# A planner that schedules forward and backward in turn, and a second layer that trails by six steps in place of five

## The chip, the cores and the metric

The kernel runs on one core of one Trainium2 chip. The metric is device time in microseconds (us) of one execution; lower is better. Medians of several executions are given; all timed runs below were in the fast state, except two single looks whose state is unknown. PE is TensorE's matrix array, PEld its weight loads, DVE is VectorE, ACT ScalarE, POOL GpSimd, SP SyncE (here it only issues DMAs).

## The reference

Two identical layers over a sequence of 2048 rows of width 512. Each layer is attention with a recurrent memory, then a dense block:

```python
x = x + A(layernorm(x)); x = x + B(layernorm(x))      # layer 0
x = x + A(layernorm(x)); x = x + B(layernorm(x))      # layer 1, same weights

def A(x, mem, Wq, Wk, Wv, Wo):                          # 64 segments of 32 rows, 32 heads of 128
    for s in range(64):
        h = concat([mem, x[32*s : 32*s+32]])            # 8 memory rows + 32
        q, k, v = h @ Wq, h @ Wk, h @ Wv
        o = softmax(mask(q @ k.T * scale)) @ v          # per head
        o = o @ Wo
        mem = o[:8]                                     # goes into the next segment
        out[32*s : 32*s+32] = o[8:]

def B(x, w1, w2): return relu(x @ w1) @ w2              # 512 -> 1376 -> 512
```

The memory makes the segments of one layer a chain: segment s+1 cannot compute its queries before segment s has been through Wo. Layer 1 needs finished rows of layer 0, but it has a chain of its own, so the two chains can run side by side.

## The kernel before

In step k the kernel works on segment k of layer 0 and segment k - DELTA of layer 1 together ("double" steps). At either end only one layer is active ("single" steps). Rows are handled in groups of 128, four segments: after the fourth segment of a group its late projection (layer 0 only), its dense block and its layer norm are due. There are 64 + DELTA steps, so DELTA single steps at each end and 64 - DELTA double ones.

No instruction order is written by hand. The kernel records all operations of all steps with engine, cost, what they read and write, and which buffers they take. A list scheduler orders them in Python while the kernel is built, and they are emitted in that order; semaphores keep the result right whatever the order, so the order is a static choice of what each engine does next.

```python
DELTA = 5
LAT = (0.26, 0.16, 0.16, 0.20, 1.70)     # PE ACT DVE POOL SP: us until others see a result
LOOK, TURN, STAY = 0.05, 0.11, 0.5       # TURN: cost of changing PE's tile form

def order(self):
    for o in reversed(self.ops):          # rank: longest path to the end, resources ignored
        o.rank = o.cost + LAT[o.eng] + max((s.rank for s in o.succs), default=0.0)
    ...
    while len(done) < len(self.ops):      # greedy: the engine that can start first, and on it,
        ...                               # of those that can start within LOOK, the highest rank
        o = max((c for c in cand[e] if c.start <= lo + LOOK),
                key=lambda c: (c.rank + (STAY if e == PE and c.tile == tile else 0.0), -c.seq))
        ...
```

The end of a step is the narrow place, where one step's memory becomes the next one's input:

```python
def project(k, act, seg):                 # OT: attention's output, transposed
    for p in range(4): ...                # Wo blocks: 8 matmuls OT x Wo into wo (tile st), per p
    ... ACT copies half of wo to wm, DVE the other half
    ... PE turns wm into columns (selm)   # "memory transposition"
    ... DVE copies the columns into HT of the next step   # "HT copy"; next K/Q matmuls wait for it
    ... DVE adds wo to the residual rows x                # two additions per active layer; not urgent
```

Attention of layer 0 needs V0, rows of values that two DMAs per step bring from vw (`V0[...] <- vw[...]`, issued by SP after all four blocks of values are evacuated, that is, copied out of PSUM). Two more DMAs fill other rows of V0 from vg, values that are computed once per group of rows. The kernel uses eight PSUM banks: five "work", one "st", two "fill"; values, dense and late projection share the two fill banks.

## Time and profile before

1972.38 us (3 runs, 1972.25 to 1975.89). I cut the trace at each HT copy. Steps 8 to 61 are double steps whose order repeats every four, because a group of rows has four segments. I call four such steps a "group", and a group is "clean" if no stretch of it ran at half PE clock.

| | before |
|---|---|
| span of the profiled run | 1973.9 us |
| PE busy / idle in the span | 1730.8 / 243.1 us |
| clean group, mean of six | 110.1 us, PE busy 101.9 |
| steps 8 to 61 | 1506.0 us |
| everything else (start, end, other steps) | 467.9 us |

The stretches view of one clean group, one line per step (32 to 35): length, then busy time of each engine, and the clock that PE was granted (1.00 is full speed).

```profile
core 0: us, PE busy (x) PEld busy (x) DVE busy (x) ACT busy (x) POOL busy (x), PEclk, DMA share, GB/s
958.20:986.50 28.30, 26.69 (x531) 19.30 (x531) 20.13 (x48) 12.84 (x30) 6.89 (x18) 1.00 0.07 14
986.50:1013.70 27.20, 25.86 (x526) 19.13 (x528) 19.64 (x45) 11.62 (x28) 6.03 (x16) 1.00 0.08 15
1013.70:1039.50 25.80, 22.63 (x480) 16.58 (x480) 19.53 (x47) 10.61 (x25) 5.99 (x16) 1.00 0.11 25
1039.50:1068.10 28.60, 26.72 (x524) 18.41 (x524) 19.32 (x44) 10.97 (x26) 6.07 (x18) 1.00 0.08 15
sum 109.90, PE 101.91 PEld 73.43 DVE 78.61 ACT 46.04 POOL 24.98; mean PE 25.48 PEld 18.36 DVE 19.65 ACT 11.51 POOL 6.25
```

PE is busy for 101.9 of 109.9 us and no other engine is close, so PE is the limit, but 8.0 us per group are idle. The third step (34) has the least work and no dense matmuls, and is idle longest. Its end, from the timeline (start, length, engine, line, operation; in brackets the idle time before it and who ended it):

```profile
1033.70 0.32 PE L660 MATMUL work_220<-ident,P_178 128*128 128x80 bf16 x4 [0.59 <-POOL P_178 L650]
...
1035.84 1.15 PE L706 MATMUL st_221<-Wo_sb,OT 128*64 128x512 bf16 x8 [0.53 <-ACT OT L469]
...
1037.03 0.37 ACT L469 CAST wm<-st_221 128x256 bf16<-128x256 f32 x1 [1.24 <-PE st_221 L706]
1037.43 0.42 DVE L471 CAST wm<-st_221 128x256 bf16<-128x256 f32 x1 [1.55 <-ACT wm L469]
...
1037.45 0.21 PE L721 MATMUL work_219<-selm,wm 128*128 128x16 bf16 x2 [0.47 <-ACT wm L469]
1037.88 0.68 DVE L746 TENSOR_TENSOR xg_72<-xg_72,st_221 16x512 f32<-16x512 f32 x1
...
1038.60 0.68 DVE L746 TENSOR_TENSOR xg_75<-xg_75,st_221 32x512 f32<-32x512 f32 x1
1039.31 0.23 DVE L730 CAST HT_172<-work_219 128x64 bf16<-128x64 f32 x1
...
1039.59 0.59 PE L567 MATMUL work_218<-HT_172,Wk_sb 128*128 128x80 bf16 x12 [0.48 <-DVE HT_172 L730]
```

PE waits for the softmax's P, then for the copies of OT, then for wm, and at last for HT. The HT copy stands behind two residual additions of 0.68 us that nobody waits for. In the fourth step PE waits for V0 (called V_181 here):

```profile
1052.51 1.03 PE L517 MATMUL fill_223<-Wv_sb,HT_172 128*64 128x512 bf16 x8
...
1054.19 1.58 SPq L540 DMA_DIRECT2D V_181<-vw  x2
...
1056.70 0.19 PE L679 MATMUL work_217<-PT,V_181 40*128 40x40 bf16 x1 [0.70 <-DMA V_181<-vw]
...
1057.67 0.19 PE L679 MATMUL work_216<-PT,V_181 40*128 40x40 bf16 x1 [0.78 <-DMA V_181<-vw]
```

From the end of the last values block to the attention that waits last it takes about 4.1 us here, and the old order had too little other work to put there.

### The profile page before, as it was taken

What the parts mean: (1) busy time and instruction counts of PE and PEld (TensorE: products, weight loads), DVE (VectorE), ACT (ScalarE), POOL (GpSimd) and SP (SyncE); (2) the same over time, 40 slices, a digit from 0 to 9 for tenths busy, and PEclk for the clock granted to TensorE, in tenths of its full rate; (3) what the DMA queues carried; (4) which work ended last, traced back from release to release, by engine and by line L of the source; (5) the groups of instructions that cost most, each with busy time, mean ns of one, the idle gap of its engine ahead of it and who ended that gap; (6) DMA issues with size and microseconds to landing.
All of it is one profiled execution on the core that took longest, in us unless ns stands there. A gap on an engine that the chain in (4) does not pass through costs nothing.

```text
span 1973.9 us, 78339 instructions
## 1 busy us (share of the span) xinstructions
PE 1730.8 (88%) x34592; PEld 1240.2 (63%) x34624; DVE 1291.7 (65%) x3103; ACT 762.6 (39%) x1843; POOL 419.4 (21%) x1171
## 2 busy tenths in 40 slices
PE   0489889999899989899999989898999999998997
PEld 0356666676566666666666666666666667666665
DVE  0245667776676767766776767776776777676654
ACT  0133334443344434444444434443443434343342
POOL 1211222221221222212221222211222222122111
PEclk9889999999999999999999999999999999999998
DMA  9210000000000000001000000000000000000000
GB/s 335 74 22 16 12 16 16 21 14 17 16 20 15 17 16 15 20 12 22 16 19 16 17 15 17 18 14 19 13 21 12 16 21 14 15 15 19 7 5 5
DMA packets 27429, 49.80 MB, mean 25 GB/s; under 512 B 8560, under 2 KB 15728, under 8 KB 27088
## 3 DMA queue, kind: packets, MB, share of 16 engines
q1 hardware_dynamic: 21520, 31.35, 7.4%
q10 hardware_dynamic: 3824, 6.78, 1.0%
q8 instruction: 271, 4.44, 0.9%
q0 software_dynamic: 1744, 6.65, 0.9%
q14 instruction: 70, 0.57, 0.1%
HBM read 21.70 MB, written 2.10 MB: 12 GB/s over the span
## 4 chain that ended last, share of the span: by engine, by line
PE 70%; DVE 10%; DMA 7%; issue 6%; ACT 4%; SPq 2%; POOL 2%; DVEq 0%; POOLq 0%; ACTq 0%
PE st_221 L706 13%; DMA V_181<-vw 7%; PE fill_222 L517 7%; PE fill_223 L517 7%; PE work_219 L567 6%; PE work_217 L567 6%; PE work_218 L567 5%; PE work_216 L567 5%; PE work_220 L567 5%; PE fill_222 L378 2%; PE fill_223 L378 2%; PE fill_223 L404 2%; SPq L540 2%; DVE wm L471 1%; ACT wm L469 1%
## 5 line engine op out<-in xcount | busy, mean ns | idle before, releaser
L567 PEld LDWEIGHTS <-Wk_sb 128*128 128x128 bf16 x8832 | 344.4, 100 | 94.1 <-issue 78.8
L567 PEld LDWEIGHTS <-Wq_sb 128*128 128x128 bf16 x8832 | 342.9, 100 | 2.4 <-issue 2.1
L706 PE MATMUL st_221<-Wo_sb,OT 128*64 128x512 bf16 x2208 | 310.9, 396 | 25.8 <-ACT OT L469 24.6
L706 PEld LDWEIGHTS <-OT 128*64 128x64 bf16 x2208 | 122.5, 111 | 121.5 <-ACT OT L469 43.0
L650 POOL TENSOR_TENSOR P_175<-es_201,sm_205 128x160 bf16<-128x160 f32 (+1 forms) x138 | 57.2, 435 | 650.1 <-DVE sm_205 L634 372.6
L753 POOL COPY OXb<-OT 128x128 bf16<-128x128 bf16 x256 | 85.9, 336 | 220.0 <-DVE OT L471 182.5
L679 PEld LDWEIGHTS <-V_181 40*128 40x128 bf16 x2048 | 49.6, 94 | 121.1 <-issue 101.9
L628 ACT ACTIVATE es_201<-es_201 128x320 f32<-128x320 f32 (+1 forms) x138 | 62.4, 452 | 99.2 <-DVE es_201 L622 99.1
L378 PEld LDWEIGHTS <-w_sb 128*128 128x128 bf16 (+1 forms) x1408 | 84.1, 102 | 8.0 <-issue 7.4
L650 POOL TENSOR_TENSOR P_176<-es_202,sm_206 128x160 bf16<-128x160 f32 (+1 forms) x138 | 61.0, 463 | 123.9 <-ACT es_201 L628 79.0
L628 ACT ACTIVATE es_202<-es_202 128x320 f32<-128x320 f32 (+1 forms) x138 | 62.2, 451 | 52.1 <-DVE es_202 L622 28.5
L517 PEld LDWEIGHTS <-HT_171 128*64 128x64 bf16 x1120 | 56.7, 110 | 38.6 <-issue 2.0
L471 DVE CAST wm<-st_221 128x256 bf16<-128x256 f32 x68 | 28.9, 424 | 79.5 <-ACT wm L469 78.7
L650 POOL TENSOR_TENSOR P_177<-es_201,sm_207 128x160 bf16<-128x160 f32 (+1 forms) x138 | 57.2, 435 | 103.4 <-DVE sm_207 L634 79.0
L517 PE MATMUL fill_223<-Wv_sb,HT_171 128*64 128x512 bf16 x592 | 77.8, 384 | 0.1
L517 PEld LDWEIGHTS <-HT_172 128*64 128x64 bf16 x1088 | 54.4, 110 | 35.8 <-issue 0.5
L352 PE MATMUL fill_222<-ident,bf_76 128*128 128x128 bf16 x136 | 13.8, 226 | 70.5 <-DVE bf_76 L347 70.5
L517 PE MATMUL fill_222<-Wv_sb,HT_172 128*64 128x512 bf16 x544 | 71.2, 383 | 0.1
L517 PE MATMUL fill_223<-Wv_sb,HT_172 128*64 128x512 bf16 x544 | 70.6, 381 | 0.1
L352 PEld LDWEIGHTS <-bf_76 128*128 128x128 bf16 x256 | 15.4, 100 | 86.7 <-DVE bf_76 L347 75.0
L469 ACT CAST wm<-st_221 128x256 bf16<-128x256 f32 x68 | 25.3, 372 | 114.8 <-PE st_221 L706 114.7
L517 PE MATMUL fill_222<-Wv_sb,HT_171 128*64 128x512 bf16 x528 | 69.1, 383 | 0.1
(299 smaller groups left out, 4230.2 us busy)
## 6 DMA issues: line engine op xcount, KB each, us to landing
V_181<-vw SPq DMA_DIRECT2D x128, 96.0 KB
V_181<-vg SPq DMA_DIRECT2D x128, 64.0 KB
Wk_sb<-in_A_Wk_dram ACTq DMA_DIRECT2D x2, 1024.0 KB
Wv_sb<-in_A_Wv_dram POOLq DMA_DIRECT2D x2, 1024.0 KB, 18.8
Wq_sb<-in_A_Wq_dram SPq DMA_DIRECT2D x2, 1024.0 KB
Wo_sb<-in_A_Wo_dram SPq DMA_DIRECT2D x2, 1024.0 KB
out_dram<-bf_76 SPq DMA_DIRECT2D x16, 128.0 KB
bf_76<-in_A_x_dram SPq DMA_DIRECT2D x15, 128.0 KB
```

The lines of the kernel that those rows point to most:

```text
L378: nc.tensor.matmul(hp[0:fs, fi * 128:(fi + 1) * 128], lhsT=w1_sb[:, c4, fc * 128:fc * 128 + fs], rhs=xnT[:, c4, :], start=(c4 == 0), stop= ...
L404: nc.tensor.matmul(yp[:, :], lhsT=hT[0:fs, fc, :], rhs=w2_sb[0:fs, fc, :], start=(fc == 0), stop=(fc == NFC - 1))
L469: nc.scalar.copy(out=out_, in_=in_)
L471: nc.vector.tensor_copy(out=out_, in_=in_)
L517: nc.tensor.matmul(vp[64 * b:64 * b + 64, :], lhsT=cols[:, c4, :], rhs=Wv_sb[:, c4, n * 512:(n + 1) * 512], start=(c4 == 0), stop=(c4 == N ...
L540: nc.sync.dma_start(out=V0[64 * b + HS:64 * b + L, :, :], in_=vw[64 * b:64 * b + L - HS, :, :])
L567: nc.tensor.matmul(qp[:, hi * 2 * L:hi * 2 * L + n], lhsT=W_sb[:, c4, h * Dh:(h + 1) * Dh], rhs=HT[:, c4, c0:c1], start=(c4 == 0), stop=(c ...
L628: nc.scalar.activation(out=e, in_=e, func=ACTF.Exp, scale=SCALE)
L650: nc.gpsimd.tensor_tensor(out=o, in0=e, in1=s.unsqueeze(3).to_broadcast([128, na, 2, L]), op=ALU.mult)
L679: nc.tensor.matmul(pv[b][:, (2 * hh + a) * L:(2 * hh + a + 1) * L], lhsT=V[R:R + KK[a], p, hh * Dh:(hh + 1) * Dh], rhs=PT[R:R + KK[a], p, ...
L706: nc.tensor.matmul(wo[64 * u:64 * u + 64, :], lhsT=OT[:, h, HS:2 * L], rhs=Wo_sb[:, h, :], start=(p == 0 and hh == 0), stop=(p == 3 and hh ...
L753: nc.gpsimd.tensor_copy(out=OXb[:, 8 * p:8 * p + 8, HS * c:HS * (c + 1)], in_=OT[:, 8 * p:8 * p + 8, 0:HS])
```

## The change

The intent: a priority that knows the resources. The new planner schedules forward with the old longest-path priorities. It then schedules that result backward from its end, honouring engines and buffer reuse, which gives each operation a latest start. Those become the priorities of the next forward pass. Six passes are made and the forward order with the smallest planned end is kept. DELTA becomes 6, so that layer 1 starts a group two steps after layer 0 has finished it. No operation, shape or buffer changes. The diff, cut to its core:

```diff
-DELTA = 5
+DELTA = 6
+PASSES = 6
...
-            o = max((c for c in cand[e] if c.start <= lo + LOOK),
-                    key=lambda c: (c.rank + (STAY if e == PE and c.tile == tile else 0.0), -c.seq))
+            o = min((c for c in cand[e] if c.start <= lo + LOOK),
+                    key=lambda c: (prio[c.seq] - (STAY if e == PE and c.tile == tile else 0.0), c.seq))
...
+                    last = pool.take(b)              # the buffer's former owner:
+                    if last is not None:
+                        o.after += last.users        # o must come after all its users
...
+    def backward(self, total):
+        ...                                          # engines filled from the end; late[] = latest start
+    def order(self):
+        ...
+        for _ in range(PASSES):
+            total = self.forward(prio)
+            if best is None or total < best[0]:
+                best = (total, [(o.start, o.seq) for o in self.ops], [(b, b.i) for b in self.bufs])
+            prio = self.backward(total)
```

## The prediction

> **What bounds the kernel now.** PE is busy 88% of 1973.9 us, VectorE 65%, ScalarE 39%, GpSimd 21% (the page). Cut at each copy of new memory columns into HT, the trace has 69 steps; steps 8 to 61 repeat in fours. A clean group (958.2 to 1068.1, by stretches) takes 109.9 us, PE busy 101.9. PE and its 8.0 us of idle are the limit. That idle, from PE's timeline:
> - V0: attention waits for the DMA from vw: 2.4 us (1.48 in the step with the late values).
> - Step ends: last Wo matmul, wm by ScalarE then VectorE, transposition, HT copy, next K matmul. 1.64 us in one step, 2.6 where two 0.68 us additions stand before the HT copy, 3.3 where a third stands before wm. Fill matmuls leave 3.3 idle.
> - The last Wo block waits for OT copies: 1.36. Transposition of P_178: 0.59..
>
> **What the change does.** No operation, shape or buffer changes; order and step number do.
> (a) DELTA 6: two more single-layer steps, one fewer double step. Single ones took 20.5 us (65, 67), a double one without dense work 25.8 (62): 2 x 20.5 - 25.8 = +15 us.
> (b) A new order, again periodic (read from the built program). Dense work reaches the step that had none; the late projection moves into the following step.
>  - V0: after the last values block PE has about 4.4, 3.0, 3.9 and 4.4 us of work before attention, where the DMA needs 4.2: idle 1.4, was 2.4.
>  - Step ends: one addition before HT in two steps, two in the others, none before wm; more fill: 2.4, was 3.3.
>  - OT: something stands between last attention and last Wo block in every step: 0.3, was 1.36. P_178: 0.3, was 0.59.
>  - Against it: 76 changes of tile form per group, were 72, at 0.11 us (K follows scores by 0.30 us, values by 0.21): +0.4. The Trainium skill, "TensorEngine Tiling (Array Packing)", Key Properties, says that changing the tiling mode drains the engine; the trace agrees (0.1 us). One step runs three attention blocks in a row (six banks wanted of five): +0.45. A transposition of normalised x stands between Wo blocks: +0.3.
>  Net -2 us per group, times 14.5: -29.
> (c) Start (75 us, mostly loading) and tail (about 15 us after the last step): -2.
>
> 1972 + 15 - 29 - 2 = about 1956 us, nearly all of it on the critical path.
>
> **Predicted: 1956 us, 1937 to 1972 eight times in ten. Faster by over 2%: 0.1; within 2%: 0.88; slower: 0.02.**
>
> **What would show it.** PE busy up by 15 to 25 us, to about 1750; its idle down from 243 to about 205. Clean group about 108 us. In the waits: Wo blocks hardly wait for OT, waits for HT shorter, V0's waits near 1.4 per group, most of it in the step after the late values. Dense matmuls in the third and fourth step of a group. Other engines' busy times up by 1 to 2%.
>
> **What would make it wrong.** If the tighter order puts the softmax chain (VectorE, ScalarE, GpSimd) on PE's path, the 2 us go and the extra step alone makes it 1975. If balancing dense work takes more of the 8 us than I count (half, say), it nears 1930. The normalisation inside a step could stall VectorE on GpSimd's power and hold up OT. Clock dips of about 1.5 us (nine steps) differ by run.

## More of the kernel before

From the page: PE's busy time, and the line of the Wo matmuls (after the bars: busy us, mean ns of one, then idle time just before them and who ended it).

```profile
PE 1730.8 (88%) x34592; PEld 1240.2 (63%) x34624; DVE 1291.7 (65%) x3103; ACT 762.6 (39%) x1843; POOL 419.4 (21%) x1171
...
L706 PE MATMUL st_221<-Wo_sb,OT 128*64 128x512 bf16 x2208 | 310.9, 396 | 25.8 <-ACT OT L469 24.6
```

## The result

1901.5 us (median of 6 runs, 1898.01 to 1906.84) against 1971.99 (6 runs): ratio 0.9644, 95% interval 0.9625 to 0.9664. Ratios here are the mean time of one kernel's fast runs over that of the other's in the same rounds, so they are not quite the ratio of the quoted medians. The change saves 70 us, 3.6%; 16 us had been predicted, and the range ended at 1937.

The page after, the same two lines:

```profile
PE 1716.8 (91%) x34902; PEld 1241.2 (65%) x34948; DVE 1292.8 (68%) x3139; ACT 777.2 (41%) x1866; POOL 419.0 (22%) x1179
...
L785 PE MATMUL st_221<-Wo_sb,OT 128*64 128x512 bf16 x2240 | 305.4, 395 | 6.5 <-ACT OT L548 5.9
```

PE makes 0.9% more matmuls and yet is busy 14 us less; the Wo blocks wait 5.9 us for OT in the whole run, where they waited 24.6. Busy time of PE is thus no measure of its work. The Trainium skill ("Perfetto Trace Analysis", Identifying the Most-Contended Engine) warns of the same figure for a related use: matmul busy share is not a good measure of how close a kernel is to the roofline, and the busy share of the weight loads is one of two measures that it puts in its place. Here the weight loads are steady, 1240.2 and 1241.2 us.

A clean group after (steps 28 to 31), by stretches:

```profile
806.30:833.30 27.00, 25.57 (x527) 18.28 (x522) 19.95 (x47) 11.88 (x28) 6.45 (x19) 1.00 0.08 15
833.30:858.90 25.60, 23.98 (x494) 17.59 (x494) 18.61 (x46) 11.10 (x27) 6.15 (x17) 1.00 0.08 15
858.90:884.50 25.60, 24.95 (x527) 19.01 (x529) 19.46 (x46) 12.04 (x28) 6.19 (x17) 1.00 0.08 17
884.50:911.00 26.50, 26.34 (x516) 18.76 (x518) 20.44 (x47) 11.89 (x27) 6.08 (x16) 1.00 0.11 25
sum 104.70, PE 100.83 PEld 73.64 DVE 78.45 ACT 46.90 POOL 24.87; mean PE 25.21 PEld 18.41 DVE 19.61 ACT 11.73 POOL 6.22
```

The group takes 104.7 us, and PE's idle time in it is 3.9 us, half of what it was. The third step, with 2.3 us more PE work than its counterpart before, is 0.2 us shorter. Its end:

```profile
878.54 0.32 PE L739 MATMUL work_220<-ident,P_178 128*128 128x80 bf16 x4
...
880.08 0.84 PE L457 MATMUL fill_223<-xnM_214,w_sb 128*128 128x128 bf16 x12
880.85 1.05 PE L785 MATMUL st_221<-Wo_sb,OT 128*64 128x512 bf16 x8
...
882.06 0.81 PE L483 MATMUL fill_222<-w_sb,hT_215 128*128 128x512 bf16 x3 [0.16 <-issue]
882.35 0.42 DVE L550 CAST wm<-st_221 128x256 bf16<-128x256 f32 x1 [1.56 <-ACT wm L548]
882.71 0.33 PE L800 MATMUL work_217<-selm,wm 128*128 128x16 bf16 x4
...
884.23 0.23 DVE L809 CAST HT_172<-work_217 128x64 bf16<-128x64 f32 x1
...
884.51 0.73 PE L646 MATMUL work_219<-HT_172,Wk_sb 128*128 128x80 bf16 x16 [0.48 <-DVE HT_172 L809]
```

The waits for P, OT and wm are gone: dense work stands in the place of the last two (fill_223 with 12 matmuls, then fill_222), and a Wo block in front of the transposition of P. The wait for HT is as it was. The "issue" of 0.16 us is no wait either: the block on fill_222 has four matmuls and the trace shows three, so one record is missing, and the gap is its time. The group shown has three such gaps, the one before two.

V0's wait in the first step of a group, which now has the late projection:

```profile
819.82 1.05 PE L596 MATMUL fill_223<-Wv_sb,HT_171 128*64 128x512 bf16 x8
...
821.53 1.59 SPq L619 DMA_DIRECT2D V_181<-vw  x2
...
824.00 0.38 PE L853 MATMUL fill_223<-wxs,selx 128*128 128x512 bf16 x1 [0.43 <-ACT wxs L850]
...
824.85 0.19 PE L758 MATMUL work_219<-PT,V_181 40*128 40x40 bf16 x1 [0.35 <-DMA V_181<-vw]
```

Where the 77.6 us between the two profiled spans (1973.9, 1896.3) come from:

| part | before | after | difference |
|---|---|---|---|
| steps 8 to 61 at the pace of their clean groups (13.5 groups of 110.07 and 105.28) | 1485.9 | 1421.3 | -64.7 |
| steps 8 to 61 above that pace | 20.1 | 6.6 | -13.5 |
| all other steps, one more of them after | 467.9 | 468.4 | +0.5 |

The second row is what the groups with a stretch of 3.4 us at half PE clock take more than clean ones: between steps 8 and 61 there are eight such stretches before and four after. Not all of it is lost at half clock. The seven groups of the kernel before that hold the eight stretches have 7.6 us more PE idle time in sum than clean ones, the four after only 0.5, and much of that idle time lies ahead of the stretches. One of them before, from the stretches view (PEclk is the third column from the right):

```profile
496.40:499.80 3.40, 1.85 (x46) 1.12 (x44) 2.84 (x9) 1.70 (x4) 2.03 (x5) 1.00 0.26 53
499.80:503.20 3.40, 3.40 (x38) 1.23 (x34) 1.27 (x3) 1.01 (x2) 1.35 (x6) 0.50 0.00 0
```

In the first 3.4 us PE was idle 1.55 us, in the next it ran at half clock.

### The profile page after: what moved, and what is told of

Same layout as the page of the kernel before. It is cut to its first block, busy times and chain, and to the rows that moved or that the text cites. A ratio compares the mean times of both kernels' runs of the same rounds, so it can differ in the third digit from the quotient of the medians.

```text
span 1896.3 us, 79089 instructions
## 1 busy us (share of the span) xinstructions
PE 1716.8 (91%) x34902; PEld 1241.2 (65%) x34948; DVE 1292.8 (68%) x3139; ACT 777.2 (41%) x1866; POOL 419.0 (22%) x1179
## 4 chain that ended last, share of the span: by engine, by line
PE 77%; DVE 7%; issue 5%; DMA 5%; ACT 3%; POOL 1%; SPq 1%; DVEq 0%; POOLq 0%; ACTq 0%
PE st_221 L785 14%; PE fill_223 L596 11%; PE work_216 L646 7%; PE work_220 L646 6%; PE work_217 L646 6%; PE work_219 L646 6%; PE work_218 L646 6%; PE fill_222 L596 5%; DMA V_181<-vw 5%; PE fill_222 L483 3%; PE fill_223 L457 2%; PE fill_222 L844 1%; SPq L619 1%; DVE wm L550 1%; PE fill_222 L457 1%
## 5 line engine op out<-in xcount | busy, mean ns | idle before, releaser
L646 PEld LDWEIGHTS <-Wk_sb 128*128 128x128 bf16 x8960 | 340.6, 99 | 75.0 <-issue 56.9
L785 PE MATMUL st_221<-Wo_sb,OT 128*64 128x512 bf16 x2240 | 305.4, 395 | 6.5 <-ACT OT L548 5.9
L729 POOL TENSOR_TENSOR P_175<-es_201,sm_205 128x160 bf16<-128x160 f32 (+1 forms) x140 | 60.0, 448 | 726.6 <-DVE sm_205 L713 579.3
L785 PEld LDWEIGHTS <-OT 128*64 128x64 bf16 x2240 | 117.4, 111 | 92.5 <-ACT OT L548 9.7
L832 POOL COPY OXb<-OT 128x128 bf16<-128x128 bf16 x256 | 79.1, 309 | 245.3 <-DVE OT L550 174.8
L596 PE MATMUL fill_223<-Wv_sb,HT_171 128*64 128x512 bf16 x776 | 101.8, 384 | 0.1
L596 PE MATMUL fill_223<-Wv_sb,HT_172 128*64 128x512 bf16 x760 | 99.3, 382 | 0.1
L729 POOL TENSOR_TENSOR P_176<-es_202,sm_206 128x160 bf16<-128x160 f32 (+1 forms) x140 | 64.0, 477 | 83.6 <-DVE sm_206 L713 79.6
L729 POOL TENSOR_TENSOR P_178<-es_202,sm_208 128x160 bf16<-128x160 f32 (+1 forms) x140 | 57.5, 432 | 107.9 <-DVE sm_208 L713 103.3
L483 PE MATMUL fill_222<-w_sb,hT_215 128*128 128x512 bf16 (+1 forms) x277 | 74.4, 381 | 6.5 <-issue 6.5
L729 POOL TENSOR_TENSOR P_177<-es_201,sm_207 128x160 bf16<-128x160 f32 (+1 forms) x140 | 57.5, 432 | 78.0 <-DVE sm_207 L713 64.9
L550 DVE CAST vw<-fill_223 128x512 bf16<-128x512 f32 x97 | 66.5, 686 | 10.0 <-PE fill_223 L596 9.8
```

The costliest lines, as they stand in the source:

```text
L483: nc.tensor.matmul(yp[:, :], lhsT=hT[0:fs, fc, :], rhs=w2_sb[0:fs, fc, :], start=(fc == 0), stop=(fc == NFC - 1))
L550: nc.vector.tensor_copy(out=out_, in_=in_)
L596: nc.tensor.matmul(vp[64 * b:64 * b + 64, :], lhsT=cols[:, c4, :], rhs=Wv_sb[:, c4, n * 512:(n + 1) * 512], start=(c4 == 0), stop=(c4 == N ...
L646: nc.tensor.matmul(qp[:, hi * 2 * L:hi * 2 * L + n], lhsT=W_sb[:, c4, h * Dh:(h + 1) * Dh], rhs=HT[:, c4, c0:c1], start=(c4 == 0), stop=(c ...
L729: nc.gpsimd.tensor_tensor(out=o, in0=e, in1=s.unsqueeze(3).to_broadcast([128, na, 2, L]), op=ALU.mult)
L785: nc.tensor.matmul(wo[64 * u:64 * u + 64, :], lhsT=OT[:, h, HS:2 * L], rhs=Wo_sb[:, h, :], start=(p == 0 and hh == 0), stop=(p == 3 and hh ...
```

## The experiments

Theories at the start. "Order": the new planner makes the gain, DELTA 6 is only a cost. "Room": DELTA 6 makes it, any planner would fill the room. "Both": each alone gains little. About the size: "restart": a wait of PE costs more than the idle time that the profile shows.

All results in one table; "clean" is the mean clean group with PE's idle time in it, "half" the half-clock stretches between steps 8 and 61, "plan" the planner's own end of schedule.

| kernel | median us | ratio to before | clean (idle) | half | plan |
|---|---|---|---|---|---|
| before (three profiles) | 1972 | 1 | 110.1, 109.9, 109.9 (8.2, 7.6, 8.0) | 8, 8, 8 | 1958.5 |
| the change (two profiles) | 1901.5, 1902.2 | 0.9644, 0.9643 | 105.3, 105.5 (4.4, 4.6) | 4, 3 | 1913.0 |
| d6_old | 1941.4 | 0.9838 | 107.9 (5.9) | 4 | 1948.5 |
| d5_new | 1949.7 | 0.9883 | 109.3 (7.5) | 0 | 1938.9 |
| p2 | 1936.0 | 0.9820 | 107.4 (5.6) | 8 | 1927.7 |
| d8_new | 2008.6 | 1.0188 | 109.4 (8.1), one group only | 20 | 1953 |
| before_htfirst | 1937.9 | 0.9828 | 109.1 (7.0) | 3 | |
| before_v0gone | 1938.0 | 0.9818 | 108.9 (7.1) | 3 | |
| before_filled | 1969.4 | 0.9987 | 110.3 (6.9) | 4 | |
| after_htfirst, again as after_htfirst2 | 1890.2, 1879.6 | 0.9584, 0.9543 | 104.3, 104.0 (3.2, 3.3) | 6, 4 | |

### DELTA alone (d6_old) and planner alone (d5_new)

```diff
 # d6_old, on the kernel before        # d5_new, on the changed kernel
-DELTA = 5                             -DELTA = 6
+DELTA = 6                             +DELTA = 5
```

> The old planner with DELTA 6 alone. Theory 'order' (the gain of 70 us is the iterated planning; the sixth step of distance is only a cost): two more single steps against one fewer double, 1975 to 1985 us. Theory 'room' (the distance gives the dense work a fourth step to lie in, and any planner fills it): 1905 to 1930, clean group of four steps near 105 us. Theory 'both' (each alone gains little, room that only the second planner uses): 1955 to 1970. The planner's own total for this order is 1948.5 against 1958.5 of before and 1913.0 of the change.

> The iterated planner with DELTA left at 5. Theory 'order': 1905 to 1925. Theory 'room': 1965 to 1980. Theory 'both': 1945 to 1960. The planner's own total is 1938.9, 19.6 below before.

Measured: 1941.4 (four runs, 1937.1 to 1945.5; ratio 0.9838, 0.981 to 0.9866) and 1949.7 (four runs, 1940.6 to 1960.6; ratio 0.9883, 0.9839 to 0.9927). d6_old fell into none of its three bands, d5_new into that of "both". Each part alone gains, 30 and 22 us, and together they gain 70, where the product of the two ratios would give 0.9723, 55 us. "Order" falls (DELTA 6 is no cost, though it adds a step), "room" falls (the old planner gets 2.1 of 4.8 us per clean group), "both" is right in kind and too strong: the clean groups gain 2.1 and 0.8 alone and 4.8 together. What d5_new gains is mostly not clean pace: over steps 8 to 61 of its profile that gives 11 us, and the disappearance of what lies above the pace (no half-clock stretch at all) 19.

The instruction order shows why the parts help each other. With DELTA 5 the first layer's dense block must be done before the next step but one begins, and the second layer's follows a step later. So d5_new, like the kernel before, has two steps without any dense work: from the first to the fourth step of a group both run 54, 54, 0 and 0 dense matmuls. Its waits for HT, wm, OT, P and V0 in the third step sum to 3.5 us. With DELTA 6 the second layer ends its group two steps after the first, and its dense block falls into that step. The change runs 32, 22, 47 and 6 dense matmuls in the four steps, the old planner with DELTA 6 11, 43, 51 and 2. So the old planner does put it there and loses P's wait, but it still lets Wo wait for OT (1.1 us per group) and adds a wait for the evacuation of vg (0.6).

### How far the planned end can be trusted (p2)

```diff
-PASSES = 6
+PASSES = 2
```

> The change with PASSES 2 in place of 6: DELTA 6, and one backward pass. The planner's own totals are 1948.5 (old order, DELTA 6), 1927.7 (this), 1913.0 (the change) and the chip gave 1941 and 1901.5 for the outer two. If the planned total tells the chip's time between orders of one DELTA, this lies near 1917 (1910 to 1925). If it does not, anywhere between 1895 and 1945.

Measured 1936.0 (four runs, 1935.2 to 1940.3), 19 us above what was expected. Of the way from d6_old to the change, the plan gains 20.8 us in the first two passes and 14.7 in the rest; the chip 5.4 and 34.5. The planned end has the right sign along this line, and the wrong size. Over all orders it does not even rank: d8_new (below) is planned shorter than the kernel before and runs 35 us longer. (d5_new is planned 9.6 us shorter than d6_old and its median is 8 us longer, but their intervals overlap.) A plan that a chip has not run says little at 1%.

### The additions behind the HT copy (before_htfirst)

```diff
-        for o in plan.order():
-            o.fn()
+        ops = plan.order()
+        ...          # cut; in words: for each HT copy, move the residual additions that stand
+                     # between the step's last Wo matmul and it to just behind it
+        for o in ops:
+            o.fn()
```

> The kernel before, its order kept, but the residual additions that stood between the step's last Wo matmul and the HT copy moved to just behind that copy. If the additions lengthen the path between steps, PE's four waits for HT in a group (0.41, 0.51, 0.80, 0.48 us) shrink to about 0.4 us in all: 1.8 us per group, about 26 us in all, 1940 to 1952. Rival: what the step ends give comes back as waits of attention for V0 or for P, since softmax and the V0 DMA then set the pace: 1962 to 1975, with V0 and P waits per group up by 1 us or more.

Measured 1937.9 (four runs, 1935.8 to 1942.0), 34 us less and a little more than expected. The third step's end, from the timeline:

```profile
910.86 1.05 PE L517 MATMUL fill<-Wv_sb,XG 128*64 128x512 bf16 x8
910.97 0.22 DVE L730 CAST HT<-work 128x64 bf16<-128x64 f32 x1 [0.30 <-PE work L721]
911.22 1.39 DVE L746 TENSOR_TENSOR xg<-xg,st 16x512 f32<-16x512 f32 x2
...
911.85 0.75 PE L567 MATMUL work<-HT,Wk_sb 128*128 128x80 bf16 x16
```

The K matmuls no longer wait for HT. Per clean group HT's waits fall from 2.19 to 0.32 us; but V0's rise from 2.45 to 3.04, so the group gains only 1.0 us, some 13 us over the steady steps. The rest lies outside the clean pace: three half-clock stretches in place of eight, and the other steps. Both the theory and its rival were half right.

### V0's wait taken away (before_v0gone)

```diff
+    nc.vector.memset(V0[:], 0.0)
...
-                nc.sync.dma_start(out=V0[64 * b + HS:64 * b + L, :, :], in_=vw[64 * b:64 * b + L - HS, :, :])
+                nc.sync.nop()
```

This computes with stale rows (it still passed the comparison, whose tolerance does not see them); the planned order is unchanged.

> Wrong result on purpose: the kernel before, order kept, the two DMAs per step from vw into V0 are not issued (V0 is cleared once), so attention does not wait for them. If a wait of PE costs just the idle time the profile shows, 2.4 us per group are saved, about 35 us: 1935 to 1942. Theory 'restart' (the first matmuls after a wait run slower too, about 0.2 us that the profile books as busy, and less idle means fewer windows at half clock): 1918 to 1932, PE busy down by 10 us or more. Rival: attention then waits for PT of the softmax instead: 1955 or more.

Measured 1938.0 (four runs, 1934.5 to 1938.9). The number is in the band of "a wait costs its idle", but the profile shows that it is there for another reason. V0's 2.45 us per group are gone, and the clean group is only 1.2 us shorter. Two lines of PE's waits over the whole run:

```profile
PE work L661 <- POOL P L651: 23.9, 51, 1.8
...
PE work L680 <- DVE PT L665: 8.6, 34, 1.3
```

In a clean group P's waits doubled (0.6 to 1.2 us), PT's came new (0.5), OT's grew (1.4 to 1.7): more than half of V0's wait had hidden the softmax behind it. Of the 34 us the clean pace explains 13.5 x 1.2 = 16; most of the rest is time above that pace (4.6 us over steps 8 to 61 in place of 20.1), with three half-clock stretches for eight. Of "restart" the fall of PE's busy time by 10 us does not show: a clean group's stays at 101.9. But the run does not test it, since new waits came for the old: 17.0 waits per clean group before, 17.3 here.

### Filling PE's waits with useless work (before_again, before_filled)

```diff
             def tr():
+                for _ in range(2 if k % 4 == 2 else 0):
+                    nc.tensor.matmul(mt[:, 64:512], lhsT=ident[:], rhs=Wo_sb[:, 0, 0:448], start=True, stop=True)
...
         def mm():                                    # attention of p
+            for i in range(8 if p == 0 and k % 4 == 3 else 0):
+                nc.tensor.matmul(pv[i % 2][:, 320:512], lhsT=ident[:], rhs=Wo_sb[:, 0, 0:192], start=True, stop=True)
```

> The kernel before, unchanged, for a second profile: how much of the half-clock windows is of the kernel and how much of one run. In the first profile 19 windows (80.1 us) ran at half clock, 8 of them between steps 8 and 61. If they belong to the kernel, again 6 to 12 between steps 8 and 61 and 1967 to 1977 us; if they were bad luck, 0 to 4 there and 1962 to 1966. Clean groups 110 us either way.

> The kernel before with useless matmuls put where PE waits: two of 448 columns before the memory transposition in every step with number 2 of four, eight of 192 columns before attention in every step with number 3. They write unused columns and nobody waits for them. Theory 'window' (PE drops to half clock for 3.4 us after a stretch of 3.4 us with more than about 1.4 us of PE idle): clean groups stay at 110 us (within 0.3), half-clock windows between steps 8 and 61 fall to 4 or fewer, 1956 to 1966 us. Rival (the half clock comes by chance or by load): the number stays at 6 to 12 and the time at 1970 or above.

The kernel before took 1971.3 us and had eight half-clock stretches between steps 8 and 61 once more: they belong to the kernel. With the filler the profiled run had four and was among the fastest (1964.6), clean groups took 110.3, as the window theory said (110 within 0.3); but the six runs gave 1969.4 (1964.6 to 1972.2; ratio 0.9987, 0.997 to 1.0004), not the 1956 to 1966 it asked for. So the count came out and the time did not. The count is not one run's accident: the mean granted clock is 0.983 to 0.988 in the six with the filler (mean 0.987) and 0.982 to 0.985 in eleven of the kernel before (mean 0.984). Filling these waits did raise the clock. An estimate from these means says that it could give 6 us at most (0.003 x 1970); 2.6 were measured, and no gain at all lies inside the interval. The filler took away only about 1.3 us of the idle time in a group.

### The change and the kernel before once more, and a better kernel (before_third, after_again, after_htfirst, after_htfirst2)

after_htfirst is the changed kernel with the same edit as before_htfirst; after_htfirst2 is the same file run again beside the changed kernel.

> The changed kernel, its order kept, with the residual additions before the HT copy moved to just behind it, as done to the kernel before (there 1938, 34 us less, of which about 1 us per clean group was seen and the rest half-clock windows). Of PE's three waits for HT per clean group (0.43, 0.76, 0.48 us) the two behind two additions in steps 0 and 2 should go, the 0.76 of step 1 should nearly stay: 0.9 us per group, 14 us in all, 1884 to 1892. Rival: step ends no longer set the pace of the changed kernel and the waits return as V0 or OT waits: 1897 to 1905.

> A third profile of the kernel before, on the chip of the two below. Steps 8 to 61 with 6 to 10 half-clock windows if 8 and 8 in the first two profiles were no accident; clean groups 109.7 to 110.1 us.

> The changed kernel unchanged, for a second profile. If the fewer half-clock windows belong to the kernel: 2 to 6 between steps 8 and 61 (first profile 4, before 8 and 8), clean groups 104.7 to 105.3 us, 1898 to 1906 us. If they were luck, 7 or more and the steady steps no closer to their clean pace than before (0.35 us per step over it) while the time stays the same.

> The changed kernel with the additions behind the HT copy once more, on the same chip as the changed kernel itself. First time 1890.2 against 1901.5 in another call. If that difference is real: 1886 to 1893, 0.5 to 0.8% under the changed kernel's median of this call. If it came from the chip: within 0.2%.

Measured: before_third 1976.0 us with eight stretches again; after_again 1902.2 (four runs) with three. So the fewer stretches are the change's, not luck; the granted clocks agree (0.985 to 0.987, against 0.980 to 0.985 of nine runs of the kernel before). after_htfirst took 1890.2 (four runs) on one chip and 1879.6 (five runs, 1878.7 to 1885.0) on the chip of after_again: 1.0% below the changed kernel there by the quotient of the two ratios, 0.9543 and 0.9643. Its clean group is 0.9 (first) and 1.6 us (second) shorter, HT's waits 0.8 us in place of 1.7. Against 14 us expected it gained 11 the first time and 23 the second; why the same file differed by 10 us, where the kernel before did not, stays open. It beats both kernels.

### More distance (d8_new)

```diff
-DELTA = 6
+DELTA = 8
```

> The iterated planner with DELTA 8: two more steps of distance than the change, but the two layers now finish their groups of 128 rows in the same step, so both dense blocks are due together again. The planner's total is 1953 (the change 1913). Theory 'where the dense work falls' (DELTA 6 pays because the second dense block comes two steps after the first and fills the steps that had none): clean group 106.5 to 108.5 us, and two more steps at about 7 us each: 1935 to 1960. Rival 'distance' (any longer distance lets the planner fill the waits): clean group 105 or less, 1905 to 1920.

Measured 2008.6 (four runs, 2004.3 to 2015.6; ratio 1.0188): slower than the kernel before, and much slower than either theory gave. "Distance" falls. At a distance of eight both layers finish a group in the same step, both dense blocks are due together, and the order has nothing to fill the end of the third step and no dense work in the fourth (32, 67, 11 and 0 dense matmuls in the four steps). Of thirteen whole groups one was clean; it took 109.4 us with 8.1 of idle. Between steps 8 and 61 there are 20 half-clock stretches. One of them, at the end of a third step, with the 3.4 us before it:

```profile
1019.20:1022.60 3.40, 1.22 (x27) 1.00 (x27) 2.75 (x6) 0.37 (x1) 0.00 (x0) 1.00 0.25 58
1022.60:1026.00 3.40, 3.40 (x57) 3.40 (x54) 2.58 (x6) 1.19 (x3) 0.55 (x1) 0.51 0.03 5
```

PE was idle 2.2 of 3.4 us, and then ran at half clock. That the fall of dense work decides, and not the distance, agrees with this; how much of the 107 us between it and the change is two more steps, bare waits and half clock I did not separate. A distance of seven was not run.

## Why the prediction was wrong

The direction, the mechanism and the places were right: dense work in the third step, the waits for OT, P, V0 and HT shrinking, PE as the limit. The step that failed is "Net -2 us per group, times 14.5: -29". Measured, clean groups are 4.8 us shorter (5.2 in the two groups shown), which makes 64.7 us, and what lies above the clean pace adds 1.0 us per group, 13.5 us, to that. Its terms, in us per clean group (the groups shown above):

| term | before | predicted | measured |
|---|---|---|---|
| V0 | 2.4 | 1.4 | 0.5 (and 0.4 for wxs in front of it) |
| step ends (wm, HT) | 3.3 | 2.4 | 1.7 |
| Wo waits for OT | 1.4 | 0.3 | 0.0 |
| transposition waits for P | 0.6 | 0.3 | 0.0 |
| third attention waits for a bank | 0 | 0.45 | 0.3 |
| normalised x in the middle of a step | 0 | 0.3 | 0.5 |
| PE's other time ("changes of tile form") | 101.9 | +0.4 | -1.1 |

- **Each wait was sized a little too long.** V0, step ends, OT and P together had been put at 4.4 us and measured 2.2 (2.6 with the wait for wxs): the planner's fill covers more of each wait than I allowed it. The group shown is one of the best: over the nine clean groups V0's waits are 0.9 us, and the four terms 2.7.
- **PE's own time went down where I had it go up.** This term has the wrong sign. The 76 changes of tile form came as counted (72 before), at about 0.1 us each; the Trainium skill ("TensorEngine Tiling (Array Packing)", Key Properties) says that changing the mode drains the engine, without a figure. But a wait takes more of PE than its idle time. In the traces the last matmul before a wait is booked 0.07 to 0.16 us past its usual slot, and a Wo block of eight takes 1.16 us from start to next start after a wait for OT, 0.99 without one. The group shown has 16 real waits before (two of 18 gaps are missing records) and 8 after (three of 11). An estimate from these: eight waits at about 0.1, three slow Wo blocks at 0.17, four more changes of form at 0.1, together -0.9; of the measured -1.1, 0.16 is the one more missing record. This is worked out from the traces; no run isolated it. The other profiles agree only roughly: with the missing records added back, a clean group's busy time is 102.2 at 17 waits (before), 101.8 at 12 (p2), 101.4 at 8 (the change) and 101.2 at 6 (after_htfirst), but 102.4 at 15.5 (before_htfirst) and at 13.6 (d6_old, which has 80 changes of form).
- **The half clock was put down to chance** ("Clock dips of about 1.5 us (nine steps) differ by run"). Three profiles of the kernel before have eight stretches each in the steady steps, two of the change four and three. In the first profiles 13.5 us of the 77.6 go with them, but only in part through the clock: about 7.1 of the 13.5 is PE idle time (7.6 less 0.5, above). Much of it was waiting for V0. In the first profile of the kernel before, PE waited 1.40 to 1.85 us for V0 just ahead of seven of the eight stretches (ahead of the other one 0.51, next to 1.04 that the profile puts down to the evacuation of vg). Two of the seven are in the fourth step of a group, where clean groups wait 1.46 us for V0 in the mean; five are in the first three steps, where the mean is 0.04 to 0.52. Yet V0 alone does not make them: before_htfirst waits longer for V0 and less for HT, and has three. The stretches follow 3.4 us windows in which PE was idle for long: in that profile the eight windows ahead of a stretch had 1.42 to 1.99 us of idle, some 420 others 1.48 at most. After the change the line is less sharp (1.14 to 1.39 ahead of a stretch, up to 1.39 elsewhere). The filler run shows that idle time in these places lowers the clock; since the line is not sharp, its sum in a window does not decide alone, and what else does stays open.
- **"2 x 20.5 - 25.8 = +15 us" was too dear.** All steps outside 8 to 61 together, one more than before, take 0.5 us more, because those steps got shorter as well (the single steps at the end but the last took 25.2, 20.5, 21.5 and 20.6 us before, 22.0, 20.7, 19.7, 20.3 and 19.4 after; and the half-clock time outside 8 to 61 fell from 52.8 to 42.6 us). (b) and (a) are not independent: DELTA 6 alone, which this sum would put at 1987, ran 30 us faster than the kernel before.

"PE busy up by 15 to 25 us" was also wrong, for the second reason and in part the third: it fell by 14 us (over steps 8 to 61 by 22, of which the 1.0 us of a clean group makes 14; outside them it rose by 8). "Idle down to about 205" was too little (179.5).

What "would make it wrong" named the right side: "If balancing dense work takes more of the 8 us than I count (half, say), it nears 1930." It took nearly half in idle time alone (8.2 to 4.4). I gave it too little weight, since I had added up single waits and trusted the sum to a few tenths each.

## What to carry to other kernels

Where two chains share one engine and each has lumps of free work, the distance between the chains decides where the lumps fall: choose it so that the lumps of one land in the bare stretches of the other, and let the scheduler see that room, because either alone got 22 and 30 of 70 us here. When sizing the removal of a wait, count the slow start and end of the neighbours as well as the gap, and look at what the windows of idle time do to the clock; and when removing one wait alone, look for the wait hidden behind it. A planner's own end of schedule is a guide for search, not a measurement: of six orders here it ranked one pair clearly wrongly, and a second one within the noise.

## What the Trainium skill lacked or had wrong

- "TensorE: Matmul & The Clock Gate", The HAM clock gate, says that PE falls to half clock after at least one idle window of about 3.4 us, and, under HAM oscillation, gives the abstract rule as no PE idle gaps over about 3.4 us. The length and the halving agree here (stretches of 3.4 us at a granted clock of 0.50). The condition does not: the longest gap of PE in the steady steps of the kernel before is 1.85 us, and windows that were idle for only 1.42 to 1.99 us in sum were followed by half clock; after the change 1.14 to 1.39 us were enough. The page does name short idle times between groups of matmuls as a second cause of such an oscillation; what it lacks is how much of them it takes.
- "TensorEngine Tiling (Array Packing)", Key Properties, says that a change of mode drains the engine, without a cost. Here it is about 0.1 us: a block of values takes 0.96 to 0.99 us when a change follows and 0.86 to 0.89 when none does.
- "Perfetto Trace Analysis" gives no figure for what a wait leaves in the neighbouring matmuls' records: here 0.07 to 0.16 us in the one before, and 0.17 us in a Wo block after, all booked as busy.
